# A gated-attention and gMLP kernel: four loads moved to ScalarE's queue, together with another layout of keys, banks and order

## The chip, the cores and the metric

The kernel runs on one core of a Trainium2 chip. The core has five engines with instruction streams of their own, each worked off in order: TensorE (PE) multiplies matrices and transposes, VectorE (DVE), ScalarE (ACT) and GpSimd (POOL) work on elements, and SyncE (SP) issues transfers. Transfers (DMAs) run on 16 DMA engines beside them. An engine waits for another one, or for a transfer, by semaphores. Matrix products are written to PSUM, which has eight banks; everything else on the core lies in SBUF.

The metric is the device time of one execution in microseconds (us). Three runs of the kernel before gave 148.49, 148.80 and 149.86 us.

## The reference

Inputs are float32: q, k, v and alpha of shape (4, 8, 768, 48), that is batch, heads, time, head dimension; the weights are w_in (384 x 1024), w_spatial (768 x 768), b_spatial (768) and w_out (512 x 384). The output has shape (4, 768, 384).

```python
for t in range(S):                                    # first part, per batch and head
    state = alpha[:, :, t, :, None] * state + einsum('bhd,bhe->bhde', k[:, :, t], v[:, :, t])
    y[:, :, t] = einsum('bhd,bhde->bhe', q[:, :, t], state)
x = y.transpose(0, 2, 1, 3).reshape(B, S, H * D)
h = maximum(x @ w_in, 0)                              # second part
u, v = h[..., :512], h[..., 512:]
v_n = (v - mean(v)) / sqrt(var(v) + 1e-6)
v_s = einsum('ts,bsd->btd', w_spatial, v_n) + b_spatial[None, :, None]
out = (u * v_s) @ w_out
```

## The kernel before

**Tiling.** Time is cut into chunks of 128 steps: 6 per batch, 24 in all. For a chunk, the kernel takes the logarithm of alpha, sums it over time with a triangular matrix on TensorE (`cum`), and exponentiates the sums on ScalarE with both signs (`einv`, `eexp`). k times the one and q times the other (`kt` on GpSimd, `qt` on VectorE) are transposed on TensorE (`trk`) and copied out of PSUM (`ev`), then multiplied with each other (`sc`: the scores of the chunk). VectorE masks the scores (`m`). The output of the chunk (`y`) is masked scores times v plus q times the state of the chunk before; the state is updated (`upd`, `z`, `S`, `sb`). The output goes through TensorE once more to be transposed (`xs`, `xt`, `xe`), and gives a column block of `xT`, the input of the second part.

Chunks 0 to 5 are treated as three pairs of 256 steps (function `pair`): one load of 384 KB brings both chunks, two consecutive steps to a partition, in runs of 384 bytes. Chunks 6 to 23 are treated singly (function `first`), with loads of 192 KB in runs of 192 bytes. For each pair or chunk there are four loads: `ac` (alpha), `kc`, `qc`, `vc`.

**The second part**, per batch: `v` (six groups of three matmuls of 512 columns, one per chunk), its mean and variance (`bn`, `rs`) and the normalised `vn`; `u` (eight groups of three matmuls of 384 columns); `s` (the product over time with w_spatial, eight groups of six matmuls); the product with u (`g`); `o` (six groups of four matmuls), and a store of 192 KB for each.

**Weights.** w_in comes as two loads (its second half, for v, first), w_spatial as three, w_out as one, of 768 KB each, into two raw buffers in turn (L1006): a third load waits until the buffer's last user, a cast to bfloat16, is done. w_spatial is transposed on TensorE (`wt`, `we`).

**What sets the order.** Every piece of work is an entry with a number. The string `PLAN` (L57 to L107) lists all numbers in the order of emission, with the engine's letter: S34 is a load's issue, Q35 its landing (nothing is emitted), P43 a TensorE entry. `P43:512:512` means: before entry 43, matmuls on a constant tile `junk` of 512 and 512 columns, whose result nobody reads (L188). `replay` (L111) emits them so; each engine then works in that order and waits where data are missing. The plan is fixed text; nothing is chosen when the kernel runs.

**Loads.** All of them are issued by SyncE, in the plan's order (L406 for pairs, L602 for chunks, L1008 for weights, L980 for stores of the output). Buffers for `ac`, `kc`, `qc` and `vc` hold three pairs each, so a load of pair or chunk pair j waits until j-3 has been used. Each DMA also takes one of eight semaphores in turn, and so waits until the DMA eight before it has landed.

**PSUM.** The eight banks are one ring: each piece of TensorE work takes the next bank (`bank`, L175), whatever it is for, and waits until that bank's last user is done.

**Keys.** `kt` keeps the scaled keys in blocks of 64 columns: for each pair of heads two blocks with data and one of zeros between (13 blocks in all, L222, L307, L311). The update of a single chunk's state (L690) then multiplies a window of 128 columns (one head's block and one of zeros) with v, twice for each pair of heads, and accumulates both in one bank. In q, and in the state's copy (L339), the two heads of a pair change places to fit.

Of the kernel before, what the change touches and what calls it, by code (L numbers as in the profile page):

```python
# [57 lines left out]
S34 S96 G0 S36 S38 Q35 D1 Q97 S100 A42 Q37 S98 P43:512:512:512:512:512:512:512:512:512:352 A104 G32 P54:512 Q33 A44  # L58
Q39 S40 P116 A55 D47 A56 P105:128 A57 G58 A45 A46 D2 Q101 S166 P50:512:96 A107 A106 P61:256 A117 D51 A118 A108 D59
A119 Q99 S102 D48 P63:512:512:512:512 A64 D121 P243:512:224 P52 D110 P125 Q41 S4 D53 D62 A126 P73:512:512:160 G120  # L60
P114 A244 D74 P76 Q167 G109 S168 P123:160 D115 D75 A49 G60 P112:512:512:192 D77 Q103 A113 P65:224 S170 D78 A124
P135:512 D66 A174 P79:96 D136 G67 Q5 S172 P138 A80 D137 G68 P69:224 A111 D70 G122 D139 P83:512:352 G71 D140 P175 G72
Q169 S9 P127 A177 A84 P81 D128 P141 A82 G129 A176 P85 Q171 S303 P186 A142 D7 G6 A86 P131 D8 A178 P143 D130 G179 A187
P87 Q173 S14 A188 D132 P90 A88 G133 D180 P145 A91 G189 D190 Q10 S305 A144 P182 D92 P184 A146 G134 P194 A185 P149
D195 G181 A183 D89 P147 P192 G191 A148 P200 G3 Q304 A193 S307 P245:128 D201 P160 A150 D202 Q15 P203 P196 D12 A13 D11
A246 D205 P156:512:512:512:512:320 S18 A93 P154 D197 A311 Q306 S309 D204 A161 G198 P152 A157 P312 D16 Q308 G199 S335
A155 P206 D151 A313 G17 Q19 A153 P210 D94 A314 A207 G315 D162 S22 P158 A316 P208 A211 P233 D317 A209 P231 D95 A163
P212 Q310 P319 D232 S337 A213 P214 D164 A234 G20 D320 Q336 P223 S370 A215 G21 D159 P217 Q23 D216 S339 P227 A218 P235
A224 P237 D219 A228 P225 A318 P229 D165 A343 Q338 D236 S341 P325 A220 D238 P321 A226 P344 Q371 D222 P259 A230 S372
D221 P251 A346 A345 D326 Q340 A24 G25 P255 S374 D322 P256 D327 A348 Q342 P260 G347 S412 D257 P239 A378 Q373 P328  # L70
G323 P241 S410 A240 D349 P379 P252 Q375 D261 A380 S414 P247 A381 D242 A329 G262 Q413 P248 A350 D253 S376 A383 P351
D249 G324 Q411 P353 P330 D352 S26 P267 A331 G258 P268 D384 Q415 S445 P357 G382 D269 P275 Q377 A418 D354 S416 P276
D359 G355 P386 Q27 D358 G356 S447 P271 D387 P419 G254 P272 A421 D277 A420 P392 A423 G422 P332 D424 P360 D273 G250
Q446 A333 S449 P426 D393 A361 P263 G274 A385 Q417 D394 P264 S477 A427 P388 P362 D265 Q448 P395 S479 A363 D31 P432
G266 D30 A396 P364 Q450 D29 A28 S481 D389 A453 D334 P397 P279 G390 Q478 A398 S572 G391 A365 P454 D433 P399 Q480 A455
D434 G278 S451 A456 A458 P408 A400 Q482 P283 D459 G425 S574 A280 D401 G457 P404 A284 Q573 P287 S604 A485 D409 G270
A405 Q452 P428 D366 P486 A288 S576 P435 A487 P461 Q575 A436 G488 S483 P291 A367 D462 A489 Q605 P295 D369 S578 A292
D429 P437 D490 A296 Q577 P467 G430 S606 A438 P406 D368 G431 A580 D469 P492 Q484 A407 S608 P581 D468 G460 P439 A582
Q579 D493 A583 S641 A585 P463 G584 P470 D464 A612 Q607 P494 D586 A471 S639 P402 G465 D495 A440 P472 Q609 G466 P613
A403 D496 S679 P588 A615 A614 G491 P299 D441 Q642 A473 S610 G587 A617 P497 G616 D589 Q640 P474 A498 S681 D618 A442  # L80
P590 P499 Q680 D591 P594 A500 S715 P620 G592 D596 A300 Q611 P501 A475 D443 S645 A476 D621 P514 Q682 P508 S643 D595
A502 P512 A503 Q716 G619 D444 S683 D515 P626 A647 P597 D504 P524 Q646 A513 S717 P528 A598 A509 Q644 D627 P540 S685
A505 P648 A687 P599 D507 Q684 P510 A600 D506 S719 P688 A649 D628 P525 Q718 A650 A690 A652 G651 S747 P541 D526 A723
P622 Q686 P529 D542 A689 G593 S749 A692 P544 D623 D530 Q720 A654 G691 P545 S751 D693 P629 D653 Q748 G624 P724 S841
P695 D511 A725 G543 P655 A630 Q750 D546 P516 S873 A726 A728 G527 P631 D696 A656 Q752 P517 S721 G625 P657 D729 P601
A632 Q842 D658 A694 G531 S843 D518 P661 A602 P701 Q874 D662 P633 G727 A755 S845 D663 P520 Q722 A634 G519 D702 S875
P756 P521 A757 Q844 D703 G659 P664 S877 P536 D522 G758 A665 Q846 P731 D635 A759 S753 P532 G660 A849 Q876 D760 P666
P697 S912 G547 P533 A667 D698 A732 Q878 P537 D534 S908 G523 P704 D538 P850 Q754 A705 P668 D603 G699 S948 A851 P762
A852 Q913 A854 G853 S847 P677 A669 D855 P706 Q909 A730 P548 G700 D678 S301 A707 D763 P733 Q949 P857 A549 D734 S879
A881 P708 D858 G735 A670 Q848 P737 S983 G535 P764 A709 D739 P863 Q302 P671 A710 S914 G736 D738 Q880 P552 S910 A636  # L90
D765 G761 P740 A672 Q984 G539 D766 P882 S950 A741 P556 A553 D864 Q915 G856 P767 S1015 A557 D865 P742 P560 A884 A768
Q911 D711 A883 S952 P673 A886 G885 P564 Q951 A743 D887 S985 A916 P769 D637 G888 P859 A561 Q1016 P675 D674 G923 S954
A770 P744 D676 A712 Q953 P777 D860 S987 A745 D638 P889 G861 Q986 A565 P771 S1019 A956 D890 A778 P779 Q955 D746 A772
S289 P917 P891 P957 A919 Q988 A918 D713 P866 S989 D714 A959 P781 A780 G920 D773 A921 Q1020 P793 S1021 A867 P797 D892
A1023 Q290 D922 P568 A774 S293 Q990 A958 P924 S1017 D776 A961 P785 D775 G960 Q1022 A782 D925 P868 S285 P786 A869
D962 G893 P794 Q294 A963 D787 G862 P798 A569 Q1018 D795 A991 P870 S570 G788 D799 S297 Q286 P926 A871 P895 D927 G796
P930 Q571 D897 P801 Q298 G894 P802 D896 P783 D932 G928 P992 D931 P789 A994 A993 P898 D803 A784 G995 P1024 A996 P966
P933 A899 D967 P790 D997 A934 G968 P809 A1025 D791 G998 A1027 P900 P810 D872 G1026 A901 P964 D1028 P999 G800 A965
P813 D1000 G792 P935 P1030 D811 A936 P814 D1031 G804 P1001 P817 D1002 G929 D815 P970 A818 P1005 D971 P1032 G1003
P942 G1029 D972 P821 G816 D1006 P805 A822 D1007 G969 P973 P937 D1033 A974 G1004 P806 D1034 A938 P975 P1008 D807 A976  # L100
P902 D943 A1009 G808 D939 P1035 A903 P1010 P977 G812 A1036 D904 P944 A978 P940 A1011 D979 P1037 P829 A1038 D945 A905
P825 D907 P1012 A826 A980 P1039 A941 D981 P1049 A1013 D982 P946 D906 A1040 D1014 P1045 A830 P1051 A947 S831 D1041
A1046 P1047 S281 P1053 S823 D1050 A1042 Q832 S558 P1057 A1052 D1044 Q282 S827 P1077 A1048 D1043 Q824 S562 P1065 Q559
# [20 lines left out]
def kernel(  # L124
# [25 lines left out]
    LN_EPS = 1e-6  # L150
    N = B * NCH

    consts = ctx.enter_context(tc.tile_pool(name="consts", bufs=1))
    IO = 3
    WK = 3
    NB, NKP = 3, 2
# [18 lines left out]
    def bank(shape):  # L175
# [5 lines left out]
        for x in shape[1:]:  # L181
            n *= x
# [901 lines left out]
```

## Time and profile before

| | |
|---|---|
| runs | 148.49, 148.80, 149.86 us (median 148.8) |
| the profiled execution's own time | 148.49 us |
| its span in the trace | 146.7 us |
| TensorE busy | 138.6 us, 94% of the span |
| VectorE, ScalarE, GpSimd busy | 120.6, 107.8, 87.1 us |
| junk matmuls (L188) | 66, from 1.3 to 28.7 us |
| read from and written to HBM | 23.60 and 4.72 MB |
| packets of the loading queue q1 | 92,960; 83.4% of the 16 engines' span |
| last load of an input issued | 110.0 us |
| last matmul ends | 143.06 us |

How to read it: busy time is the time in which an engine had an instruction under way; a matmul's end is modelled, so matmuls that follow each other overlap in their rows, and "0.49 us for three" in the chain of work is their pace. A row of 40 digits cuts the span (or the window asked for) into equal slices, in tenths busy. The chain of work is followed back from the last instruction to whatever released each step. In a list by time, the columns are start, length, engine, line, operation, output and input, count, and in brackets how long the engine had waited before it and for whom. "SPq" is SyncE's queue.

### The profile page before, as it was taken

The page shows a single profiled execution, that of the slowest core. Times are in us where ns is not written, and L with a number is a line of the kernel's source. Part 1 is how long each engine was busy: PE and PEld are TensorE (multiplying, and loading weights), DVE is VectorE, ACT ScalarE, POOL GpSimd, SP SyncE. Part 2 cuts the span into 40 slices and gives each one's busy share as a digit, 9 for nine tenths or more (in the row PEclk, how much of TensorE's full clock was granted, in tenths as well). Part 3 has the DMA queues.
Part 4 walks back from the last instruction along what each step waited for, and adds up shares of the span by engine and source line. Part 5 has one row for each costly group of instructions (what it writes and reads, how often), then busy time and mean ns, then how long its engine had stood idle before and what let it go on. Part 6 is the DMA issues. An engine that isn't in the chain of part 4 may idle for free.

```text
span 146.7 us, 4486 instructions
## 1 busy us (share of the span) xinstructions
PE 138.6 (94%) x1702; PEld 92.3 (63%) x1715; DVE 120.6 (82%) x260; ACT 107.8 (73%) x271; POOL 87.1 (59%) x148
## 2 busy tenths in 40 slices
PE   6999999999999999995998999999999999999990
PEld 3567776676666666773666577666667766566550
DVE  6578989979999899994977898988989999767820
ACT  3595779988984599995996889999948548860160
POOL 5726487574258959773139987853597994004320
PEclk9999999999999999999999999999999999999998
DMA  4999998978997999997998999999998000063384
GB/s 109 268 261 263 330 259 245 332 183 210 312 216 151 267 208 199 197 197 141 191 213 163 221 194 206 186 210 188 202 222 258 22 0 0 4 242 138 135 293 161
DMA packets 93014, 28.61 MB, mean 195 GB/s; under 512 B 87872, under 2 KB 91456, under 8 KB 92992
## 3 DMA queue, kind: packets, MB, share of 16 engines
q1 hardware_dynamic: 92960, 28.32, 83.4%
q8 instruction: 13, 0.21, 0.6%
q14 instruction: 9, 0.07, 0.2%
q0 software_dynamic: 32, 0.00, 0.0%
HBM read 23.60 MB, written 4.72 MB: 193 GB/s over the span
## 4 chain that ended last, share of the span: by engine, by line
PE 64%; DMA 12%; DVE 8%; ACT 5%; POOL 4%; issue 3%; SPq 1%; DVEq 0%; ACTq 0%; POOLq 0%
PE bank L778 38%; DMA qc<-in_q_dram 7%; PE bank L188 6%; DMA raw_w<-in_moe_w_spatial_dram 5%; PE bank L704 2%; POOL gT L933 2%; PE bank L672 2%; PE bank L732 2%; PE bank L361 2%; PE bank L674 2%; PE bank L690 1%; DVE qt L656 1%; PE bank L492 1%; PE bank L428 1%; SPq L602 1%
## 5 line engine op out<-in xcount | busy, mean ns | idle before, releaser
L778 PE MATMUL bank<-w_spT,vn 128*128 128x384 bf16 x192 | 36.3, 326 | 0.0
L933 POOL TENSOR_TENSOR gT<-vsb,uT 128x384 bf16<-128x384 f32 x28 | 25.8, 932 | 16.1 <-DVE vsb L920 15.5
L778 PEld LDWEIGHTS <-vn 128*128 128x128 bf16 x192 | 17.3, 97 | 10.0 <-issue 0.2
L715 DVE TENSOR_TENSOR ptm<-bank,mask 128x512 bf16<-128x512 f32 x36 | 22.8, 681 | 0.5 <-PE bank L704 0.5
L646 POOL TENSOR_TENSOR kt<-kc,binv 128x384 bf16<-128x384 f32 x18 | 16.7, 928 | 7.4 <-ACT bc L641 4.4
L920 DVE TENSOR_TENSOR vsb<-bank,bsp_bc 128x384 f32<-128x384 f32 x31 | 16.7, 552 | 3.8 <-PE bank L778 2.8
L778 PE MATMUL bank<-xT,w_in 128*128 128x384 bf16 x96 | 19.2, 327 | 0.0
L778 PE MATMUL bank<-w_out_sb,gT 128*128 128x384 bf16 x96 | 18.4, 326 | 0.1
L778 PE MATMUL bank<-w_in,xT 128*128 128x512 bf16 x59 | 17.1, 379 | 1.0 <-issue 0.5
L332 POOL TENSOR_TENSOR state<-state,bc 128x192 f32<-128x192 f32 x20 | 10.2, 511 | 8.2 <-DVE state L327 4.9
L198 POOL CAST sbd<-state 64x192 bf16<-64x192 f32 x38 | 12.9, 340 | 2.0
L196 ACT COPY xT<-bank 128x384 bf16<-128x384 bf16 x24 | 11.7, 487 | 3.0 <-PE bank L361 2.4
L839 DVE BATCH_NORM_STATS2 stats<-v_sb 128x6 f32<-128x512 bf16 x20 | 13.6, 682 | 0.3 <-ACT v_sb L202 0.3
L202 ACT ACTIVATE v_sb<-bank 128x512 bf16<-128x512 f32 x20 | 11.7, 598 | 2.6 <-PE bank L778 2.2
L656 DVE TENSOR_TENSOR qt<-qc,bank 128x384 bf16<-128x384 f32 x18 | 9.8, 548 | 4.4 <-DMA qc<-in_q_dram 2.9
L188 PE MATMUL bank<-junk 128*128 128x384 bf16 (+5 forms) x66 | 11.8, 313 | 1.3 <-DVE junk L231 1.3
L198 DVE COPY kqT<-bank 128x1024 bf16<-128x1024 bf16 (+1 forms) x19 | 11.6, 614 | 1.5 <-PE bank L674 0.5
L196 ACT COPY o_sb<-bank 128x384 f32<-128x384 f32 x9 | 4.3, 480 | 11.4 <-PE bank L778 11.4
L778 PEld LDWEIGHTS <-w_in 128*128 128x128 bf16 x96 | 8.7, 98 | 6.1
L778 PEld LDWEIGHTS <-gT 128*128 128x128 bf16 x96 | 9.0, 97 | 5.4 <-issue 0.3
L196 ACT CAST x_sb<-bank 128x384 bf16<-128x384 f32 x24 | 11.6, 488 | 1.0 <-PE bank L732 0.5
L871 DVE TENSOR_SCALAR vn<-v_sb,mvs,rstd 128x512 bf16<-128x512 bf16 x24 | 10.6, 467 | 2.0 <-ACT rstd L864 1.9
(124 smaller groups left out, 299.1 us busy)
## 6 DMA issues: line engine op xcount, KB each, us to landing
ac<-in_alpha_dram SPq DMA_DIRECT2D x18, 192.0 KB, 4.1
kc<-in_k_dram SPq DMA_DIRECT2D x18, 192.0 KB, 3.9
qc<-in_q_dram SPq DMA_DIRECT2D x18, 192.0 KB, 3.8
vc<-in_v_dram SPq DMA_DIRECT2D x18, 192.0 KB, 4.2
raw_w<-in_moe_w_spatial_dram SPq DMA_DIRECT2D x3, 768.0 KB, 7.6
out_dram<-raw_w SPq DMA_DIRECT2D x12, 192.0 KB, 2.3
out_dram<-o_sb SPq DMA_DIRECT2D x9, 192.0 KB, 2.4
raw_w<-in_moe_w_in_dram SPq DMA_DIRECT2D x2, 768.0 KB, 7.6
```

The source lines that it names most:

```text
L188: nc.tensor.matmul(out=flat[:, 0:n], lhsT=junk[:, 0:128], rhs=junk[:, 0:n], start=True, stop=True)
L196: nc.scalar.copy(out=out, in_=in_)
L198: ENG[eng].tensor_copy(out=out, in_=in_)
L202: nc.scalar.activation(out=out, in_=in_, func=AF.Relu)
L646: ENG[eng].tensor_mul(out=k_blocks(kt3)[:, :, :, 0:D], in0=quad(st["kc"]), in1=st["binv"])
L656: nc.vector.tensor_mul(out=qt[:, :, ::-1, 0:D], in0=quad(st["qc"]), in1=st["cv"])
L715: nc.vector.tensor_tensor(out=st["ptm"][:, s], in0=st[f"pt{s}"], in1=mask4, op=ALU.mult)
L778: return lambda ps: nc.tensor.matmul(out=out(ps), lhsT=lhsT(), rhs=rhs(), start=start, stop=stop)
L839: nc.vector.bn_stats(out=stats, in_=d["v_sb"][:, tt, :])
L871: nc.vector.tensor_scalar(out=d["vn"][:, t, :], in0=d["v_sb"][:, t, :], scalar1=d["mvs"][:, t, 0:1], scalar2=d["rstd"][:, t:t + 1], op0=AL ...
L920: nc.vector.tensor_tensor(out=hold["vs"], in0=ps[:, 0:TH], in1=bsp_bc[:, th, :], op=ALU.add)
L933: ENG[eng].tensor_tensor(out=bt[b]["gT"][:, dsl, cols], in0=hold["vs"], in1=bt[b]["uT"][:, dsl, cols], op=ALU.mult)
```

## The change

Four things change.

1. For the pairs 1 and 2, the loads of k and v are issued by ScalarE, on a hardware queue of its own. All other loads stay on SyncE. In ScalarE's program the issue of k1 stands after the table load, those of v1 and k2 after the first logarithm, and that of v2 between the two exponentials of the first half of pair 0, with a wait for k1's landing (the DMA eight before it).
2. Keys are kept without zero blocks, two heads side by side as in q. The state update of a single chunk writes the two halves of the partitions separately, with 64 columns of keys each.
3. The one ring of eight banks becomes three: two banks for sums, updates and outputs (`a`), two for the transposes and scores (`p`), four for the second part and the pairs (`p2`).
4. `PLAN` is another text: the order of all entries, the engines of some, and the junk (12,032 columns in place of 16,224). All 12 loads of the pairs stand ahead of the first load of w_in, where 9 stood before. Eight stores, where there were three, stand ahead of the last input load. The sums of pair 1 stand behind the first scores instead of ahead of them.

Besides: `xT` and `w_spT` are laid out with time running through, the bias is kept in float32, some buffers come from pools in turn instead of being named, and the squares for the variance (four chunks) go to a buffer of their own. Of the entries with a choice of engines, four `u` evictions go from ScalarE to VectorE, two `ev` and one bias copy too, two casts go from VectorE to GpSimd, one `we` from VectorE to ScalarE, one `sb` from GpSimd to VectorE and one `vbp` from ScalarE to GpSimd.

```diff
 PLAN = """
-S34 S96 G0 S36 S38 Q35 D1 Q97 S100 A42 Q37 S98 P43:512:512:512:512:512:512:512:512:512:352 A104 G32 P54:512 Q33 A44
...
+G32 Q33 G0 S34 S36 Q35 S38 S96 S40 Q37 S98 D1 S100 S166 A42 Q39 S102 D2 S170
+P43:384:384:384:384:384:384:384:384:384:384:384:384 S168 G3 Q97 S4 P54:384 A46 A44 S172 A45 S303 G47 A57 A55 D48 Q41
...
-    banks = [pp.tile([128, 512], FP32, name=f"bank{n}") for n in range(8)]
-    turn = [0, 0]
-    def bank(shape):
-        flat = banks[turn[0] % 8]
-        turn[0] += 1
...
+    pp_a = ctx.enter_context(tc.tile_pool(name="pp_a", bufs=NA, space=bass.MemoryType.PSUM))
+    pp_p = ctx.enter_context(tc.tile_pool(name="pp_p", bufs=NP, space=bass.MemoryType.PSUM))
+    pp_2 = ctx.enter_context(tc.tile_pool(name="pp_2", bufs=8 - NA - NP, space=bass.MemoryType.PSUM))
+    def bank(pool, shape, dtype, **kw):
+        t = pool.tile(shape, dtype, **kw)
...
-    bsp_bc = consts.tile([128, 2, TH], BF16, name="bsp_bc")
+    bsp_bc = consts.tile([128, 2, TH], FP32, name="bsp_bc")
-    w_spT = consts.tile([128, NT, NT, 128], BF16, name="w_spT")
+    w_spT = consts.tile([128, NT, S], BF16, name="w_spT")
...
-    ktp_bufs = [consts.tile([128, 2, 3 * HP + 1, 64], BF16, name=f"kt{i}") for i in range(NKP)]
+    lap_bufs, ktp_bufs, qtp_bufs = [
+        [consts.tile([128, 2, H, 64], BF16, name=f"{x}{i}") for i in range(NKP)] for x in ("la", "kt", "qt")]
...
-    ring = Ring(8)
+    rings = {"a": Ring(NA), "p": Ring(NP), "p2": Ring(8 - NA - NP)}
...
-                nc.sync.dma_start(
+                (nc.scalar if j and name in ("kc", "vc") else nc.sync).dma_start(
                     out=t.rearrange("p h a d -> p h (a d)"),
                     in_=src[b, :, t0:t0 + 2 * C, :].rearrange("h (p a) d -> p h (a d)", a=2))
...
                 for hp in range(HP):
                     for s in range(2):
                         nc.tensor.matmul(
-                            out=st["tp"][:, hp, :], lhsT=k_window(kt3, hp, 2 - 2 * s),
-                            rhs=st["vb"][:, 2 * hp + s, :], start=(s == 0), stop=(s == 1))
+                            out=st["tp"][64 * s:64 * s + 64, hp, :], lhsT=kt[:, hp, s, :],
+                            rhs=st["vb"][:, 2 * hp + s, :], start=True, stop=True)
...
-        d["xT"] = batch.tile([128, NCH, KS, C], BF16, name="xT")
+        d["xT"] = batch.tile([128, KS, S], BF16, name="xT")
```

## The prediction

> **What bounds the kernel now.** I read the page first: its busy shares, its row of slices, its chain. Then, stage by stage, the loading queue's own instructions, TensorE in order of time, and the transfers in the first 24 us.
>
> ```profile
> span 146.7 us, 4486 instructions
> PE 138.6 (94%) x1702; PEld 92.3 (63%) x1715; DVE 120.6 (82%) x260; ACT 107.8 (73%) x271; POOL 87.1 (59%) x148
> PE   6999999999999999995998999999999999999990
> PEclk9999999999999999999999999999999999999998
> DMA  4999998978997999997998999999998000063384
> PE 64%; DMA 12%; DVE 8%; ACT 5%; POOL 4%; issue 3%; SPq 1%; DVEq 0%; ACTq 0%; POOLq 0%
> ```
>
> TensorE is busy from the second slice on at an unchanged clock, and the transfers are busy until slice 31: two bounds lie close together. A busy TensorE may still run junk or crawl, so I added up its real work by the chain's rows: three 512- or four 384-column matmuls 0.65 us, three 384-column ones 0.49, eight transposes 0.44, three 0.18, and so on. All of it but the junk is 127.2 us, of which 78 are the 112 large groups u, v, s, o. The last matmul ends at 143.06, so 15.8 us are lost. The transposes of each finished chunk (L361) show where: clock time minus the real work ordered before them is 10.5 us at chunk 3, 11.8 at chunk 5, 12.7 at chunk 9, 15.6 at chunk 13 and 15.3 at chunk 23.
>
> ```profile
> 64.55 0.34 PE L361 MATMUL bank<-ident,x_sb 128*128 128x128 bf16 x3
> ...
> 68.36 0.36 PE L690 MATMUL bank<-vb,kt 128*128 128x48 bf16 x8 [1.09 <-POOL vb L198]
> ...
> 69.67 0.38 PE L672 MATMUL bank<-ident,kt 128*128 128x128 bf16 x4 [0.46 <-DVE qt L656]
> ...
> 79.47 0.40 PE L674 MATMUL bank<-ident,qt 128*128 128x128 bf16 x4 [0.30 <-DVE qt L656]
> ```
>
> The reader is to see two TensorE waits in brackets between 64 and 70 us; behind both stands a load (the chain has `qc` loads of 5.16 and 4.87 us here). So the losses are: 10.5 us of start, 1.3 around 28 us (junk while the second half of w_in is fetched), 0.6 by chunk 7, about 2.9 between 60 and 81 us to late loads, and nothing afterwards. From 81 us on the kernel is bound by TensorE alone.
>
> **The start, where the named edit lies.** The loading queue and the transfers:
>
> ```profile
> 0.74 1.06 SPq L406 DMA_DIRECT2D ac<-in_alpha_dram  x2
> 1.85 1.19 SPq L406 DMA_DIRECT2D kc<-in_k_dram  x1
> 3.08 2.74 SPq L406 DMA_DIRECT2D qc<-in_q_dram  x2
> 5.87 1.44 SPq L406 DMA_DIRECT2D kc<-in_k_dram  x1
> 7.35 1.44 SPq L406 DMA_DIRECT2D vc<-in_v_dram  x1
> ```
>
> ```profile
> GB/s 0 0 0 74 234 325 310 263 261 261 259 262 262 261 261 258 261 262 261 261 261 262 260 280 254 281 323 381 383 332 297 267 265 255 198 282 246 57 191 356
> ```
>
> The first two issues take 0.53 us each, later ones 1.4. The second fence is the window of 0 to 24 us in 40 slices: flat at 261 GB/s while the 384 KB loads run. 393,216 bytes at 261 GB/s are 1.51 us, which is also the spacing of the landings (users start at 4.62, 6.14 and 7.68 us). So issue is held back by the transfers; SyncE is not the limit.
>
> *The four issues.* ScalarE now issues k of pair 1 behind its table load (2.01 us), v1 and k2 behind its first logarithm (5.46), and v2 between the first two exponentials, after a wait for k1. Each costs ScalarE between 0.53 and 1.45 us, so 2.1 to 5.8 in all. Queued behind them are the exponentials of pair 0, and behind those the products for k and q, the transposes and the scores. I take 0.53 for the first three and 1.2 for v2, whose queue is not empty: the first exponential's copy would end near 9.2 us in place of 8.46. Cover: q of pair 0 lands about 10, and its product waits for that anyway. If the cover goes, 3 us.
>
> *Sharing.* What the second queue takes, the first lacks. Sharing half and half, with 1.51 us a load: q0 lands near 10.0 (now at most 9.8), alpha1 13.1 (now 6.1), v0 16.1 (now 13.6), q1 18.3 (now at most 10.8), v1 about 11 (now 17.9). If ScalarE's queue yields, alpha1 lands at 9.2 and v0 at 10.7. By the changed order, TensorE has the sums of pair 1 (they need alpha1) ahead of state update 0, scores 0/1 and output 0. Output 0 then comes at about 19.2 instead of 15.96, covered partly by the junk that both versions put there. Moreover all 12 pair loads now stand ahead of the first half of w_in, where 9 do today: it lands 4.5 us later, near 23.4, and after its casts (0.50 to 0.80) the first v group starts at about 25.5 behind 13.5 us of real work. That is a loss of 12.0, against 10.3 at v's first group now (21.63, work 11.3). Bounds for this stage: 0 (the queue yields) to +3.2 (all of output 0's delay stays). I take **+1.6**.
>
> [...]
>
> *u's wait.* The second half of w_in comes no later than now (16.5 against 16 load units ahead of its end), and with v pushed back TensorE reaches u at about 30 us. The junk and wait of 1.3 us there fall away: **-1.0**; bounds -1.3 to 0.
>
> **The rest of the diff.** *Loads from 26 us on.* The first third of w_spatial waits for the casts of w_in, done near 25 instead of 21.6, and SyncE's in-order queue holds chunk 6's k and q behind it: a transfer gap of about 1.6 us that today's order does not have. Between 60 and 81 us TensorE already waits for loads, so the gap shows there: 0 to +1.6, I take **+1.2**. Eight stores instead of three stand ahead of the last input load (3.8 us, at 196,608 bytes and 261 GB/s); today the last loads are issued at 110.0 and chunk 23 ends at 124.3, so this is covered up to some 5 us.
>
> *Banks.* One ring of 8 banks becomes rings of 2, 2 and 4. A chunk takes 3 + 3 + 4.7 banks in some 4.3 us, so a bank comes round every 2.9, 2.9 and 3.7 us instead of 3.2. Held longest: scores, 0.26 and two masks of 0.68 on VectorE; transposes, 0.44 and 0.68; the sums, 0.29 + 0.50 + 0.50 + 0.55. All are shorter than 2.9 but only by a microsecond, and VectorE is 82% busy. Bounds: 0 to +5 (0.3 for each of 18 single chunks). The nearest row is the stretch from 81 us on, where no bank costs anything: **+0.5**.
>
> *Assignments.* VectorE gains four u evictions (0.54 each), one state copy pair (1.5), two transposed copies and a bias, and loses two casts and a w_spT copy: +3.3 us, where it has 26 idle. 0 to +3.3; I take 0. *Forms with one answer:* keys without the zero blocks (update matmuls 0.20 us per chunk against 16 in 0.36 for the half-width form: -0.4 to 0), memsets of `kt` 0.27 shorter twice beside an idle VectorE, a float32 bias (the `qt` row with a float32 operand is 0.548, `vsb` 0.552), new layouts of `xT` and `w_spT`: 0 together. The junk falls from 16,224 to 12,032 columns, about 1.8 us, but at the start, where TensorE waits for loads either way: 0.
>
> **Sum.** 1.6 - 1.0 + 1.2 + 0.5 = +2.3. The profiled execution took 148.49 us (span 146.7 and 1.8 around it), so 150.8; against the median of 148.8, +1.3%. The runs spread over 0.9%, so about 1% is what a measurement can tell from no change.
>
> **Rivals.** (1) *Faster, by the second queue's own rate.* If 261 GB/s is one queue's limit and not the DMA engines', two queues reach up to the 383 GB/s of the w_in slices: 12 loads end 18.1 - 12.3 = 5.8 us sooner. It decides above about 348 GB/s (261 x 12/9), where the first half of w_in lands no later than now; a third of the gain stays, as the matmuls' order is fixed: -2.0, 146.5. Against it: the same queue reaches 383 with longer runs, so the run length seems to limit. (2) *No difference.* The later start is paid back between 60 and 81 us, where TensorE waits 2.9 us for loads that come no later in absolute time: 148.8. It decides if the gap at 26 us closes. (3) *Much slower, by banks.* Scores and transposes of successive chunks block each other in a ring of two as VectorE runs late; at 0.3 us for each of 18 chunks and +1 at the start, 154.8. For it: VectorE at 9.1 to 9.4 of 10 us from 40 to 60 us. (4) *ScalarE blocked at its issues*, 5.8 us, of which some 3 uncovered: 151 to 152, inside the forecast's own range.
>
> **Numbers.** Forecast (with 4) 0.40, rival 1 0.13, rival 2 0.27, rival 3 0.20. The forecast's own case reaches from 149.8 to 152.5. For 8 in 10 the range takes in rival 2, most of rival 3 and the upper edge of rival 1: 147.4 to 155.8. Faster by over 1% is rival 1, 0.13; within 1%, rival 2 and the forecast's lowest edge, 0.29; slower, 0.58.
>
> **What would show it.** Two hardware queues with 261 GB/s in sum in the first 18 us (rival 1: above 348); the first v group near 25 us; no junk wait before u; the loss at chunk 5 near 12.5, at chunk 13 near 17.5, flat from there. PE waits named for DVE masks or ACT evictions all along would be rival 3. I would be wrong if start-up delays of 2 us never reach the end, or if the order of the changed kernel leaves TensorE less idle between 60 and 81 us than I allow.

## The result, and the profile after

The changed kernel takes 160.13 us (median of four runs, 158.63 to 160.25) against 149.33 for the kernel before beside it (148.49 to 150.63): a ratio of 1.069, 95% interval 1.059 to 1.080. That is 10.8 us slower; 150.8 was forecast, and 155.8 was the upper end of the range. The profiled execution took 158.63 us, 1.8 of it outside its span of 156.9.

From the page of the changed kernel, the lines that answer to those of before, with the granted clock's row, the rate of the transfers and the two hardware queues (their columns: packets, MB, share of 16 engines' span):

```profile
span 156.9 us, 4387 instructions
PE 146.8 (94%) x1674; PEld 94.6 (60%) x1687; DVE 121.8 (78%) x266; ACT 105.8 (67%) x264; POOL 86.8 (55%) x149
...
PE   6597899999899899999999999999999999999990
...
PEclk9969755559999999999999999999999999999999
DMA  4999994055899979999989999899699700450054
GB/s 116 270 261 261 265 323 168 2 181 128 231 261 216 198 151 189 187 276 205 198 166 194 197 195 199 178 249 221 129 231 270 161 6 0 170 214 22 22 213 168
...
q1 hardware_dynamic: 88800, 26.75, 73.3%
q10 hardware_dynamic: 4160, 1.57, 4.7%
...
PE 79%; DVE 7%; issue 7%; POOL 4%; ACT 1%; ACTq 0%; POOLq 0%
```

Each digit stands for 3.9 us. TensorE is again 94% busy, of a span 10 us longer, though the changed kernel does no more with it. The PEclk row says why a part of that is not work: the clock is at a half from slice 5 to slice 8 (slices count from 0), where the row of before had nines. And the DMA row has a hole at slice 7 (2 GB/s) that before did not have. Both lie in the first 36 us; from slice 9 on the two pages look alike.

The same stretch in windows of 4 us (columns: window, its length, then busy time and instructions of PE, PEld, DVE, ACT and POOL, the granted clock, the DMA share in units where 1.28 is the flat start, GB/s):

```profile
12.00:16.00 4.00, 2.78 (x44) 1.45 (x42) 2.27 (x5) 2.86 (x8) 0.74 (x2) 1.00 1.28 261
16.00:20.00 4.00, 3.73 (x78) 3.06 (x78) 2.92 (x6) 1.51 (x5) 3.16 (x7) 0.71 1.27 267
20.00:24.00 4.00, 4.00 (x59) 2.79 (x57) 2.22 (x6) 2.24 (x5) 1.33 (x3) 0.50 1.11 334
24.00:28.00 4.00, 4.00 (x65) 2.80 (x63) 2.43 (x6) 2.39 (x6) 1.97 (x4) 0.50 0.34 120
28.00:32.00 4.00, 4.00 (x56) 2.99 (x58) 2.28 (x6) 1.00 (x2) 3.88 (x8) 0.50 0.03 6
```

In 12 to 16 us TensorE has 1.2 us without work; from 17.7 us on the clock is at a half, until 34.7. TensorE then counts as fully busy, while VectorE is busy for 2.2 to 2.4 of 4 us, ScalarE for 1.0 to 2.4 and GpSimd for 1.3 to 3.9. TensorE waits for none of them there, so it is its pace at half the clock that sets these 17 us. The same TensorE entries, from the transposes of pair 1's keys (entry 112) to the first v group, can be held against the run e5 below, in which the clock is whole (the first line is the changed kernel, the second e5; columns as above):

```profile
17.63:33.22 15.59, 15.59 (x234) 11.70 (x232) 9.56 (x22) 7.27 (x17) 8.86 (x18) 0.50 0.59 163
19.19:29.08 9.89, 9.89 (x235) 7.62 (x233) 9.28 (x21) 7.24 (x17) 6.58 (x14) 1.00 0.70 208
```

Both times TensorE is busy throughout; at half the clock the same work takes 5.7 us more.

What TensorE waited for at 15 us, and when SyncE could go on, in the lists by time of GpSimd, TensorE and SyncE:

```profile
15.26 0.95 POOL L193 CAST vbp<-vc 128x384 bf16<-128x384 f32 x2 [6.51 <-DMA vc<-in_v_dram]
```

```profile
15.82 0.18 PE L509 MATMUL tp<-vbp,kt 64*64 64x48 bf16 x1 [1.21 <-POOL vbp L193]
...
33.22 1.49 PE L759 MATMUL ps<-w_in,xT 128*128 128x512 bf16 x3
```

```profile
17.85 1.88 SPq L585 DMA_DIRECT2D ac<-in_alpha_dram  x1
19.77 1.44 SPq L986 DMA_DIRECT2D raw_w<-in_moe_w_in_dram  x1
31.74 0.37 SPq L986 DMA_DIRECT2D raw_w<-in_moe_w_spatial_dram  x1
```

The cast of v0 started at 15.26 us, as soon as v0 had landed (13.6 before), and the first group of v started at 33.22 us (21.63 before). The issue of w_spatial's first third, which waits for the casts of w_in's first half, came at 31.74 (22.36 before); SyncE stood for 10.4 us.

**Where the 10 us went.** The measure is the prediction's: the time of a finished chunk's transposes (L361 before, L346 after), less the real work ordered ahead of it. In the kernels with the changed order, that work is 6.7 us ahead of chunk 0, 18.0 ahead of chunk 4 and 110.3 ahead of chunk 23; in those with the old order 9.0, 20.8 and 109.0. Losses, in us, of the profiled execution of every kernel in this study:

| kernel | ratio | clock | first v group | chunk 0 | chunk 4 | chunk 23 |
|---|---|---|---|---|---|---|
| before | 1 | 1.00 | 21.6 | 10.5 | 11.8 | 15.3 |
| after | 1.069 | 0.935 | 33.2 | 14.0 | 20.8 | 25.4 |
| after, junk throughout (e1) | 1.072 | 0.997 | 32.1 | 13.8 | 18.9 | 23.6 |
| after, loads on SyncE (e2) | 1.015 | 0.999 | 25.0 | 8.9 | 11.8 | 17.6 |
| before, the named edit (e3) | 1.003 | 1.00 | 23.2 | 11.8 | 13.4 | 14.4 |
| before, less junk (e4) | 1.012 | 0.953 | 24.0 | 11.5 | 13.6 | 15.2 |
| after, junk in waits (e5) | 1.046 | 0.989 | 29.1 | 14.5 | 15.9 | 20.5 |
| after, later issues (e6) | - | 0.967 | 29.7 | 9.7 | 17.8 | 22.5 |
| after, casts earlier (e7) | - | 0.922 | 34.8 | 15.6 | 23.5 | 28.1 |
| after on SyncE, w_in first (e8) | 1.043 | 0.977 | 27.4 | 8.9 | 15.4 | 20.0 |
| after on SyncE, less junk (e9) | 1.049 | 0.933 | 28.5 | 10.7 | 16.3 | 20.8 |
| before, early issues (e10) | 1.024 | 0.987 | 26.4 | 15.3 | 16.5 | 17.4 |
| after, later issues and junk (e11) | 1.032 | 0.998 | 27.4 | 9.8 | 14.2 | 18.9 |
| e8 with junk in waits (e12) | 1.022 | 0.995 | 25.6 | 9.2 | 12.5 | 17.1 |

The 10.1 us between the first two rows arise in three places: 3.5 by chunk 0 (14.0 against 10.5), 5.5 from there to chunk 4 (+6.8 against +1.3), 1.1 in all the rest (+4.6 against +3.5). The kernel is decided by its first 39 us. For e6 and e7 no ratio is given, since their executions differ among themselves by more than the rest; their rows are of executions of 155.69 and 161.32 us. The row of before is from the same set of runs as the row of after, at 148.49 us, while the medians of before beside e1 to e12 were 1.0 to 1.6 us faster, and no trace of before was taken there. Rows of the old order (e3, e4, e10) are therefore to be held against an estimated 13.7 to 14.3 at chunk 23.

### The profile page after: what moved, and what is told of

The parts are those of the page before. It is cut to its first block, busy times and chain, and to the rows that moved or that the text cites. A ratio compares the mean times of both kernels' runs of the same rounds, so it can differ in the third digit from the quotient of the medians.

```text
span 156.9 us, 4387 instructions
## 1 busy us (share of the span) xinstructions
PE 146.8 (94%) x1674; PEld 94.6 (60%) x1687; DVE 121.8 (78%) x266; ACT 105.8 (67%) x264; POOL 86.8 (55%) x149
## 4 chain that ended last, share of the span: by engine, by line
PE 79%; DVE 7%; issue 7%; POOL 4%; ACT 1%; ACTq 0%; POOLq 0%
PE ps L759 47%; PE pt L655 5%; PE pt L685 4%; PE y L346 3%; PE y L556 3%; PE ps L478 2%; PE tp L671 2%; PE y L713 2%; PE cum L604 2%; POOL mask L243 2%; PE y L707 2%; PE tp L509 2%; DVE vn L851 1%; PE pt L529 1%; PE ps L413 1%
## 5 line engine op out<-in xcount | busy, mean ns | idle before, releaser
L759 PE MATMUL ps<-w_spT,vn 128*128 128x384 bf16 x192 | 36.2, 326 | 0.0
L912 POOL TENSOR_TENSOR gT<-vsb,uT 128x384 bf16<-128x384 f32 x28 | 25.7, 927 | 15.7 <-DVE vsb L899 15.1
L628 POOL TENSOR_TENSOR kt<-kc,binv 128x384 bf16<-128x384 f32 x18 | 16.4, 914 | 15.3 <-ACT binv L616 15.0
L696 DVE TENSOR_TENSOR ptm<-pt,mask 128x512 bf16<-128x512 f32 x36 | 23.9, 681 | 0.3 <-PE pt L685 0.2
L317 POOL TENSOR_TENSOR state<-state,bc 128x192 f32<-128x192 f32 x20 | 10.4, 522 | 19.4 <-DVE state L312 15.9
L759 PE MATMUL ps<-xT,w_in 128*128 128x384 bf16 x96 | 19.7, 326 | 0.5 <-ACT xT L191 0.4
L899 DVE TENSOR_TENSOR vsb<-ps,bsp_bc 128x384 f32<-128x384 f32 x31 | 16.5, 550 | 3.4 <-PE ps L759 2.9
L759 PE MATMUL ps<-w_in,xT 128*128 128x512 bf16 x59 | 18.0, 392 | 0.8 <-ACT xT L191 0.2
L759 PE MATMUL ps<-w_out_sb,gT 128*128 128x384 bf16 x96 | 18.4, 326 | 0.1
L191 ACT CAST x_sb<-y 128x384 bf16<-128x384 f32 x24 | 11.6, 481 | 9.6 <-PE y L713 5.0
L821 DVE BATCH_NORM_STATS2 stats<-v_sb 128x6 f32<-128x512 bf16 x20 | 13.7, 684 | 1.8 <-ACT v_sb L197 1.7
L191 ACT COPY xT<-y 128x384 bf16<-128x384 bf16 x24 | 11.5, 480 | 4.3 <-PE y L346 3.9
L197 ACT ACTIVATE v_sb<-ps 128x512 bf16<-128x512 f32 x20 | 11.9, 597 | 2.3 <-PE ps L759 2.2
L638 DVE TENSOR_TENSOR qt<-qc,cum 128x384 bf16<-128x384 f32 x18 | 9.9, 548 | 2.3 <-ACT cum L633 2.0
L540 DVE TENSOR_TENSOR ptm<-pt,mask 128x512 bf16<-128x512 f32 x12 | 7.7, 686 | 3.7 <-PE pt L529 3.7
```

The source lines that it names most:

```text
L191: nc.scalar.copy(out=out, in_=in_)
L197: nc.scalar.activation(out=out, in_=in_, func=AF.Relu)
L317: ENG[eng].tensor_tensor(out=st["state"], in0=st["state"], in1=st["bc"][:, :, None].to_broadcast([128, HP, D]), op=ALU.mult)
L628: ENG[eng].tensor_mul(out=kt[:, :, :, 0:D], in0=quad(st["kc"]), in1=st["binv"])
L638: nc.vector.tensor_mul(out=qt[:, :, :, 0:D], in0=quad(st["qc"]), in1=st["cv"])
L696: nc.vector.tensor_tensor(out=st["ptm"][:, s], in0=st[f"pt{s}"], in1=mask4, op=ALU.mult)
```

## The experiments

The kernel before ran beside each set, at medians of 146.9 to 147.5 us. Four theories were there to be told apart: TensorE's waits let the clock fall (clock; A in the expectations of e1 to e4); the loads of the second queue make others land late (late landing; B); the banks and the new order cost time all along (C); SyncE's wait and the hole in the transfers move everything after them (gap).

**e1: junk wherever the clock had fallen.** 46 matmuls of 384 columns, at 14 places of the plan up to the third pair's scores; for example

```diff
-P112:384:384:384:384:256 ... P79 A119
+P112:384:384:384:384:256 ... P79:384:384:384 A119
...
-P135 A84 G111 P175 Q169
+P135:384:384:384 A84 G111 P175:384:384:384 Q169
```

> The changed kernel with 46 more junk matmuls of 384 columns in its first 35 entries of TensorE, where its trace has waits (8 before the first sums, 7 before the first state update, the rest two to four at a time); nothing else differs. Theory A (clock): most of the 10 us are TensorE at half its clock from 17.7 to 34.7 us, which began because TensorE was left waiting in two stretches. Then the granted clock stays at 1.0 from some 5 us on, the first third of w_spatial is issued near 25 us instead of 31.7, and the time is 149 to 152 us. Theory B (late loads: the loads on the second queue push v of pair 0 and alpha of pair 1 back by 3 to 7 us): the landings stay as they are, so 156 to 160 us whatever the clock does. Theory C (banks and order): 156 to 160 us as well, with the loss spread over the whole run.

Measured: 157.46 us (156.81 to 158.03), ratio 1.072 (1.066 to 1.077). From its page and its TensorE list:

```profile
PEclk9999999999999999999999999999999999999998
```

```profile
32.06 0.81 PE L759 MATMUL ps<-w_in,xT 128*128 128x512 bf16 x3
```

The clock held, and the time did not move. That looked like an end of the clock theory, and was not: the junk itself now stood in TensorE's way. 27 of the 46 matmuls stand behind the wait for v0, where the chain of work has TensorE alone; at their pace (three in 0.49 us) they are 4.4 us. The run exchanged one cost for another; e5 leaves that cost out.

**e2: the four loads back on SyncE.**

```diff
-                (nc.scalar if j and name in ("kc", "vc") else nc.sync).dma_start(
+                nc.sync.dma_start(
```

> The changed kernel with its four loads issued by SyncE again, at the same places of the plan; all else as changed. Theory B: alpha of pair 0 lands near 4.6 us again instead of 5.5, v of pair 0 near 11 instead of 15.3, and most of the loss is gone: 149 to 152 us. Theory A: the time follows the clock; if TensorE's wait before the first state update goes, the clock stays up and the time is 150 to 153; if a drop remains, 155 or more. Theory C: 157 to 160 us.

Measured: 148.93 us (148.71 to 150.84), ratio 1.015 (1.008 to 1.023). In GpSimd's and TensorE's lists:

```profile
10.36 0.96 POOL L193 CAST vbp<-vc 128x384 bf16<-128x384 f32 x2 [1.83 <-DMA vc<-in_v_dram]
```

```profile
24.98 0.81 PE L759 MATMUL ps<-w_in,xT 128*128 128x512 bf16 x3 [0.85 <-POOL w_in L193]
```

v0 is there at 10.4 us instead of 15.3, with the same order of everything else. TensorE's waits stay short and the clock holds with the changed kernel's own junk. So most of the loss, 1.069 to 1.015, hangs on the named edit; the rest of the diff, banks and order included, costs 1.5% when all loads are on SyncE, so theory C can't be the main cause. (The profile is that of the slowest of the four runs, 150.84 us.)

**e3: the named edit alone, in the kernel before.** The same line the other way round, in the old order.

> The kernel before with the named edit alone: k and v of pairs 1 and 2 issued by ScalarE at the same places of its plan. Theory A: its junk still fills TensorE's waits, the clock stays at 1.0, and the time is within 1.5 us of before. Theory B: the second queue delays the loads that are needed first, and the time grows by 3 us or more. Theory C: no difference.

Measured: 147.41 us (146.96 to 148.24, ten runs), ratio 1.0031 (1.0006 to 1.0055). The same edit costs 5% in one order and 0.3% in the other. ScalarE's issues (its queue, by time) tell what differs; first e3, then the changed kernel:

```profile
4.38 0.44 ACTq L406 DMA_DIRECT2D kc<-in_k_dram  x1
10.14 0.43 ACTq L406 DMA_DIRECT2D vc<-in_v_dram  x1
13.07 0.37 ACTq L406 DMA_DIRECT2D kc<-in_k_dram  x1
15.74 0.37 ACTq L406 DMA_DIRECT2D vc<-in_v_dram  x1
```

```profile
0.77 0.48 ACTq L391 DMA_DIRECT2D kc<-in_k_dram  x1
5.53 0.37 ACTq L391 DMA_DIRECT2D vc<-in_v_dram  x1
5.93 0.63 ACTq L391 DMA_DIRECT2D kc<-in_k_dram  x1
7.21 2.46 ACTq L391 DMA_DIRECT2D vc<-in_v_dram  x1
```

In the old order the issues stand between ScalarE's other work and so come one at a time up to 15.7 us; in the new one all four are in the queue by 9.7 us, beside the loads that are wanted first.

**e4: the kernel before without its junk,** but for the first group (for example `P63:512:512:512:512` becomes `P63`).

> The kernel before without its junk matmuls, except the first group of 4,960 columns: 11,264 columns fewer, nothing else differs. Theory A: TensorE's waits are left bare, the clock falls to a half somewhere between 9 and 30 us, and the time grows by 3 to 10 us. Theories B and C (and the forecast, which priced missing junk at nothing): within 1 us of before.

Measured: 148.77 us (148.42 to 149.33), ratio 1.012 (1.008 to 1.016); the clock is at a half for 13.7 us, mean 0.953. The clock fell as theory A had it, but the time grew by less than its 3 to 10 us: in the old order 13.7 us of half clock cost some 1.8 us, 0.13 for each. A likely reason, which no run tests, is that the junk that is gone no longer stands in the way, and that the loads that TensorE then waits for come no later.

**e5: junk only where TensorE waits.**

```diff
-P43:384:384:384:384:384:384:384:384:384:384:384:384 S168
+P43:384:384:384:384:384:384:384:384:384:384:384:384:384:384:384 S168
...
-P50:384:384:384:384:384:384:384:96 P52 A51
+P50:384:384:384:384:384:384:384:96 P52:384:384 A51
...
-P65 A117
+P65:384:384:384:384:384:384:384 A117
```

> The changed kernel with 12 more junk matmuls of 384 columns, only where TensorE waited (3 before the first cumulative sum, 2 before q's first transposes, 7 before the first state update), none behind it. Late-landing theory (k1, v1, k2 and v2 on the second queue take half of the transfer rate, v0 lands near 15.3 instead of 10.4 us, and everything up to the first v group is queued behind it): v0 lands at 15-15.7 again, the first w_spatial load is issued at 29-30.5 (31.7 after, 25.0 with the loads on SyncE), the first v group is at 30.5-32, the time 156-158. Clock theory (the half clock between 17.7 and 34.7 makes the lateness): the clock stays at 1.0 and the first v group is at 25-27, the time 150-152.

Measured: 153.74 us (152.92 to 154.45), ratio 1.046 (1.039 to 1.053). From the page, GpSimd's and TensorE's lists:

```profile
PEclk9999599999999999999999999999999999999999
```

```profile
15.71 0.96 POOL L193 CAST vbp<-vc 128x384 bf16<-128x384 f32 x2 [7.07 <-DMA vc<-in_v_dram]
```

```profile
29.08 0.81 PE L759 MATMUL ps<-w_in,xT 128*128 128x512 bf16 x3
```

The result lies between the two expectations, so both causes are at work. v0 is as late as in the changed kernel, and the loss at chunk 0 is not smaller (14.5). But from chunk 0 to chunk 4 it grows by 1.4 us in place of 6.8. Twelve matmuls on a constant took the ratio from 1.069 to 1.046. What is left against e2 (1.046 to 1.015) is put down to the late landing, with 3.4 us of half clock still in it.

**e6: the four issues later in ScalarE's order.**

```diff
-... Q37 S98 D1 S100 S166 A42 Q39 S102 D2 S170
+... Q37 D1 S100 S166 A42 S98 Q39 D2 S170
...
-S9 A56 D58 ... A104 P245 ... A117 G109
+S9 A56 S102 D58 ... A104 S168 P245 ... A117 S172 G109
```

> The changed kernel with the same four loads on ScalarE's queue, but each issued later in ScalarE's order: k1 behind the first logarithm, v1 behind the first pair's last exponential, k2 behind the second logarithm, v2 behind the second pair's second exponential of the negated sums. Late-landing theory: what competes with alpha1 and v0 is gone, v0 lands at 11-13, the first w_spatial load is issued at 25.5-28, the first v group at 26-28.5, the time 150.5-154. If the second queue itself or ScalarE's issuing costs the time: the time stays at 156-160.

Measured: 151.49 to 155.76 us, median 155.23. v0 lands at 12.0 as expected, and the loss at chunk 0 is 9.7. Then the third pair's alpha is late: its logarithm starts at 19.6 us (16.0 in e2), TensorE waits 2.67 us for it, and the clock is at a half from 22.3 to 32.6 us. The four executions sort by the clock: 155.69, 154.76 and 155.76 us at 0.967, 151.49 at 0.988. The expected time came in one of four; e11 is the same kernel with the wait filled.

**e7: the casts of w_in's first half earlier.**

```diff
-... Q169 D136 ... D128 Q5 A86 D180
+... Q169 D136 ... D128 Q5 G6 A8 D7 A86 D180
...
-G133 D183 Q304 P200 D7 A8 G6 P192
+G133 D183 Q304 P200 P192
```

> The changed kernel with one edit: the three casts of w_in's first half stand earlier in the order of GpSimd, ScalarE and VectorE (ahead of the second pair's state update, of chunk 1's second activations copy and of the third pair's q). Load-gap theory (the empty stretch of the transfers from 25 to 32 us, while SyncE waits for these casts, is what moves the end): the first w_spatial load is issued at 25-27.5, the gap shrinks to under 2 us, the time falls to 152-155. TensorE-order theory (the first v group stands behind the second and third pair's work in TensorE's own order, and that work is late): the gap shrinks as well, but the first v group stays at 32.5-34 and the time at 157-160.

Measured: 153.94 to 161.32 us, median 158.67. SyncE's and TensorE's lists:

```profile
27.71 0.37 SPq L986 DMA_DIRECT2D raw_w<-in_moe_w_spatial_dram  x1
```

```profile
34.77 0.63 PE L759 MATMUL ps<-w_in,xT 128*128 128x512 bf16 x1
```

w_spatial is issued 4 us sooner, the transfers run again from 28 us, and in this execution (161.32 us) nothing is gained: the first v group is no earlier, because TensorE's own order has it behind the second and third pair. At one and the same clock, 0.931, e7 took 160.11 us and the changed kernel 160.17. Both speak against the gap theory; of the one execution with a whole clock there is no trace. The four executions give a price of the clock instead, in one and the same program, though only as a correlation: 153.94 us at 0.998, 157.24 at 0.952, 160.11 at 0.931, 161.32 at 0.922. From the first to the last that is 7.4 us for 24 more microseconds at a half (0.998 of a span of 152.1 leaves 0.6 us, 0.922 of 159.5 leaves 24.9): 0.30 us for each. The stretch shown above, 15.59 against 9.89 us, gives 0.37. The figure of 0.6 in the expectation of e9 below was an error of mine by a factor of two.

**e8, e12: loads on SyncE, w_in at its old place in the queue; then with junk in the waits.**

```diff
-... Q39 S102 D2 S170 ... S168 G3 Q97 S4 P54:384 ... S172 A45 S303 ... S9 A56
+... Q39 S102 S4 D2 S170 ... S168 G3 Q97 P54:384 ... S172 S9 A45 S303 ... A56
...
-P184 G179 D190 P141:384:288 D132
+P184:384:384:384:384:384:384:384:384:384 G179 D190 P141:384:288:384:384 D132
```

(The second half of the diff is e12's alone.)

> The changed kernel with all loads on SyncE and, besides, w_in's two halves back at their old places of SyncE's queue (the first ahead of q2, k2 and v2, the second ahead of chunk 6's alpha). If the place of w_in is what is left of the loss of the kernel with the loads on SyncE (148.9, ratio 1.015): the second half lands near 27-28 instead of 29.9, the ratio to the kernel before is 1.000-1.007. If the rings of PSUM or the order of the engines are what is left: it stays at 1.011-1.020.

> The changed kernel with all loads on SyncE, w_in's two halves at their old places of SyncE's queue, and 11 more junk matmuls of 384 columns where TensorE waited in the run without them (9 before the third pair's first transposes of q, 2 before chunk 2's output). Two-part theory: the clock holds at 0.99 or more, the first v group comes at 24.5-26 (27.4 at the half clock), the time is 148.3-150.5 (153.2 without the junk). If w_in's place in the queue were all that is left of the loss with the loads on SyncE, the first v group would be at 22-23.5 and the time at 146.8-148. If the clock isn't the cause of the 153.2, it stays at 152.5-154.

Measured: e8 153.19 us (152.65 to 154.04), ratio 1.043 (1.037 to 1.049); e12 150.55 us (150.37 to 150.71), ratio 1.022 (1.016 to 1.029). e8 lies outside both of its expectations: q2 and k2 now stand behind w_in, TensorE waits 1.34 us for q2's product at 20.5 us, and the clock falls to a half from 23.2 to 30.0. With the wait filled it stays up and 2.6 us come back; the time is just above what was expected. Against e2 (1.015) the old place of w_in gains nothing in the new order, so what the 1.5% of e2 consists of isn't settled by these two.

**e9: loads on SyncE, only the first group of junk.** The diff is e2's, and all junk behind the first group goes.

> The changed kernel with all loads on SyncE and of its junk only the first group of 12 matmuls. Theory of two parts (loads that land late make TensorE wait and work late, about 4 us at the full clock; the waits then let the clock fall to a half, about 0.6 us of time for each microsecond of half clock): with the loads back on SyncE TensorE waits less, but without junk the clock falls all the same, to 0.94-0.98, and the time is 151-154 (148.9 with the junk). Rival, that the junk matters only beside the second queue: the clock stays at 0.99 or more, the time at 148.5-149.5.

Measured: 154.51 us (153.97 to 155.23), ratio 1.049 (1.044 to 1.054). From the page:

```profile
PEclk9985555599999999999999999999999999999999
```

Clock (0.933) and time lie just beyond the expected ends. The clock falls without any second queue, for 20.5 us, and costs 5.6 us against e2 (4.9 by the ratios): 0.24 to 0.27 us for each. So the two causes are separate ones; the second queue is only one way to make TensorE wait.

**e10: the kernel before, its four issues as early as in the changed kernel** (e3's line, and the plan changed so):

```diff
-... Q97 S100 A42 Q37 S98 P43:512 ... Q33 A44 Q39 S40 ... Q99 S102 D48 ... G109 S168 P123 ... Q5 S172 P138
+... Q97 S100 S98 A42 S102 S168 Q37 P43:512 ... Q33 A44 S172 Q39 S40 ... Q99 D48 ... G109 P123 ... Q5 P138
```

> The kernel before with the four loads on ScalarE's queue, issued as early as the changed kernel does it (k1 ahead of the first logarithm, v1 and k2 right behind it, v2 behind the first exponential of the negated sums), all else as before. Two-part theory: the second queue takes half of the transfer rate from the first microsecond, v0 lands at 14.5-17 and alpha2 late, the junk of the kernel before holds the clock at 0.98 or more, so only the first part of the loss appears: time 149-152, ratio 1.015-1.035. Rival, that the order of the kernel before takes the landing of these loads as it comes (ratio 1.003 with the four issues later): 147-148.

Measured: 150.69 us (150.65 to 151.83), ratio 1.024 (1.020 to 1.029), where e3 with later issues had 1.003. GpSimd's list and the page:

```profile
18.01 0.50 POOL L198 CAST vbp<-vc 128x384 bf16<-128x384 f32 x1 [4.54 <-DMA vc<-in_v_dram]
```

```profile
PEclk9969999999999999999999999999999999999999
```

v0 is even later than in the changed kernel and than expected, the clock is almost whole behind the old kernel's junk (3.4 us at a half, mean 0.987), and 2.1% are lost by the moment of the issues alone, what follows from it included. Against e3, in the same order, the loss is 3.1 us larger at chunk 4 (16.5, 13.4) and still 3.0 at chunk 23 (17.4, 14.4): none of this lateness is given back.

**e11: e6 with its waits filled** (e6's diff, `P65:384:384`, and 15 times `:384` at `P175`).

> The changed kernel with its four loads on ScalarE's queue issued later in ScalarE's order, as in the run with later issues, and 17 more junk matmuls of 384 columns only where TensorE waited in that run (2 before the first state update, 15 before the third pair's first cumulative sums). Two-part theory: alpha2 still lands near 19.5, the clock holds at 0.985 or more, the first w_spatial load is issued at 26-27.5 (28.4 without the junk, 31.7 after), the first v group is at 26.5-28.5, the time 149.5-152. If the clock isn't the cause: 153.5-156 whatever the clock does.

Measured: 152.08 us (151.97 to 152.40), ratio 1.032 (1.028 to 1.037). ScalarE's and TensorE's lists:

```profile
19.62 0.84 ACT L402 ACTIVATE la<-ac 128x768 bf16<-128x768 f32 x1 [2.66 <-DMA ac<-in_alpha_dram]
```

```profile
27.42 0.81 PE L759 MATMUL ps<-w_in,xT 128*128 128x512 bf16 x3
```

The time is at the upper edge. The first logarithms are as early as in e2 (4.63 and 10.03 us), alpha2 as late as in e6, the clock at 0.998: 3 us better than e6's median, and 3 us short of e2, because alpha2 now pays for the second queue in place of v0. At each moment of the issues that was tried, some load of SyncE's gave way.

No kernel of these beats the kernel before.

## Why the prediction was wrong

The sign was right and the landing of the loads nearly so; the size was not, and the step that failed is a clause: "The junk falls from 16,224 to 12,032 columns, about 1.8 us, but at the start, where TensorE waits for loads either way: 0." Beside the loads that landed late, the thinner junk let the clock fall to a half, and that was not worth 0: e5, which only fills the waits, takes 3.4 us off by the ratios (2.3% of 147) and 6.4 off the median. The second step is a term that was too small: the late landing, taken at +1.6, is worth some 3.8 (e5 against e2, below).

- **The two queues.** "261 GB/s in sum in the first 18 us" was measured: 261 to 270 in each slice from 4 to 20 us, with the second queue at work. The first rival (146.5) needed 348 and falls.
- **The four issues.** 0.48, 0.37, 0.63 and 2.46 us, 3.9 in all, inside the 2.1 to 5.8; the one taken at 1.2, behind a queue that isn't empty, was twice that, and ScalarE's first `eexp` (`ps`, L438) ended at 10.2 us instead of 9.2.
- **Sharing.** alpha1 landed at 11.5 us (issued at 3.1, and 8.4 to landing; 13.1 was worked out), and v0's cast started at 15.26 (16.1). Output 0 started at 18.72 (19.2). So far the working by halves, which was an estimate, is good to 1.6 us.
- **From there to the first v group**: forecast 25.5, measured 33.2. This is where it broke. The forecast let w_in's landing set that group. With the loads on SyncE and the clock whole it does: in e2 the group started at 24.98, after a wait of 0.85 for a cast of w_in. In the changed kernel TensorE had the whole second and third pair ahead of it, and walked through them at half the clock. e5 takes 4 us of this away with twelve junk matmuls and no other edit. Junk was counted as time and columns; what it does for the clock was not in the sum, though the page of before had it in view: a whole clock beside 66 junk matmuls.
- **"+1.6", bounds 0 to +3.2**: the term was worked out at v's first group, as a loss of 12.0 against 10.3. There 33.2 less the prediction's 13.5 us of work is a loss of 19.7, so 9.4 above before, with the half clock in it. The loss by chunk 0 alone rose by 3.5, just above the upper bound. The cover named for it, junk that both versions hold at that place, isn't there: TensorE stood idle 1.2 of the 4 us before v0.
- **u's wait, -1.0, and loads from 26 us on, +1.2.** The wait before u is gone. The hole in the transfers came, not for 1.6 us but for nearly 7 (19 GB/s from 25 to 32 us), since the casts it hangs on stand behind the late pairs in three engines' orders. But e7, which fills a good part of it, is no faster than the changed kernel at the same clock (160.11 and 160.17 us at 0.931): by that the hole was a sign, not the cause. No run sizes this term alone.
- **Banks, +0.5.** From chunk 13 to chunk 23 the loss grows by 1.1 (24.3 to 25.4), where before it fell by 0.3. That is 1.4 for banks, the eight stores and the rest together; no run takes them apart, and e2 bounds the rest of the diff as a whole at 1.5%. The third rival's time (154.8) lay nearer than the forecast, but by a mechanism that the trace doesn't show: in that stretch the list of TensorE's waits is empty, as it is before.
- **The second rival, no difference,** says that a late start is paid back between 60 and 81 us. Of that the old order does a little: from before to e3 chunk 4 is 1.6 us later, the median time only 0.5, and TensorE's idle time between chunks 5 and 13 falls from 2.5 to 0.2 us (the trace of before comes from another set of runs than e3's, so this 1 us is an estimate). Once these waits are used up it does nothing more (e10 against e3). The new order does none: from chunk 4 to chunk 23 the loss grows by 4.5 to 4.7 us in nine of the ten kernels with it, however late they start (5.8 in e2). That the same edit cost 0.3% in the old order and 5% in the new has three reasons, then, as far as runs in two orders may be added: the moment of the four issues (e10 against e3, 2.1%), the thinner junk with its fallen clock (after against e5, 2.3%), and the microsecond given back.

Put together: 20.5 us of half clock (7.4 to 10.8 and 17.7 to 34.7) at the 0.30 us of e7 make 6.1 us; e5 less 1.0 for its own 3.4 us of half clock, 152.7 us, stands 3.8 above e2 for the late landing; e2 stands 2.2 above before (1.5%) for the rest. That is 12.1, where 10.8 were measured. By the 0.37 of the stretch it would be 1.4 more. The changed kernel was not run again beside the experiments, where the kernel before was some 2 us faster than beside it, so whether the terms overlap or the two sets of runs differ stays open; what the 1.5% of e2 is made of does as well.

## What to carry to other kernels

Here a second queue added no rate (261 to 270 GB/s in sum from 4 to 20 us, where the one queue of before had 261 while the 384 KB loads ran): it only decided which loads came later, so before moving a load, list what will stand beside it in the first microseconds and which of these TensorE needs first. Junk matmuls are part of a kernel's timing and not of its work: whoever changes the order of the loads must look anew at where TensorE waits and put the junk there, and only there, since junk behind a wait can cost what it saves (e1: the clock at 0.997, and 1.072). And before counting on a late start being paid back, look whether the order that you move into still has waits of its own further on to absorb it.

## What the runs showed of the hardware

- *The clock fell after stretches in which TensorE was partly idle.* The clock was at a half for 3.41 and 17.07 us (after), 3.41 (e5), 10.24 (e6) and 6.82 (e8): one, five, one, three and two times 3.41. In the 3.41 us ahead of each fall TensorE was busy for 1.76 and 1.93 us (after), 2.10 (e5), 1.84 (e6) and 1.74 (e8), so 39 to 49% idle, with longest single waits of 1.2 to 2.7 us. Over as long a time with 2.32 us busy (e6, from 15.50 us), 2.56 (e2, from 22.55) and 2.03 (e2, from 29.37) it stayed up, so these rows give no dividing line. At the start the row can't be read as the pace: in the changed kernel it says 1.00 from 1 to 4 us, where junk matmuls of 384 columns start 0.32 us apart (1.61 to 3.54 us), against 0.17 from 16.86 to 17.36, also at 1.00.
- *In one stretch being busy did not bring it back.* From 17.66 to 34.73 us TensorE of the changed kernel shows as busy without a gap (3.41 of each 3.41 us), mostly with products of 48 to 128 columns, and the clock stays at 0.50. In the last 3.41 of these, from 31.31, the first 512-column group of v runs (33.22), and from 34.73 the clock reads 1.00. From 7.42 to 10.83 us, also busy throughout and at 0.50, eight junk matmuls ran, seven of 384 columns and one of 96 (2.50 us), beside smaller work, and from 10.83 the clock read 1.00. What brought it back in either case no run shows.
- *One issue held ScalarE for 1.96 us.* In the changed kernel three of the four issues took ScalarE 0.37 to 0.63 us. That of v2, at 7.21 us, took 2.46, while v1 and k2 had not landed (12.1 and 15.4 us); the next activation stood behind it for 1.96 us. In e10 the issue of v2 took 1.20, in e3, at 15.74 us, 0.37.
